# Retention and a gated feed-forward block on one core: start-up laid out by what has landed, filler matmuls, q's squares by way of DRAM, decays per piece, a reordered tail

## The chip, the core and the metric

The kernel runs on one core of a Trainium2 chip. The metric is the device time of one execution in microseconds (us). The kernel before takes 1089.98 us, the median of three runs (1087.69 to 1090.47). One more execution was profiled, and every line of profile below comes from it.

## The reference

All arrays are float32. Eight batches of eight heads, 576 positions, head size 64, go through a decayed causal attention without softmax, and the result, as 4608 tokens of 512 features, goes through a feed-forward block with a gate.

```python
scores = q @ k.T / sqrt(64)
gamma = 1 - 2 ** (-5 - head)
ret = scores * where(i >= j, gamma ** (i - j), 0)
x = (ret @ v)              # heads side by side: (4608, 512)
h = x @ w_in               # w_in (512, 2048)
g = h * erf(softplus(h))
out = g @ w_out            # w_out (2048, 512)
```

## The kernel before, in words

**Attention** works in 40 *pieces*: each batch's 576 positions are cut into four pieces of 128 and one of 64. A piece has three stages. T(i) (`transposes`) turns q and k: TensorE transposes each pair of heads against the identity into PSUM (L296) and ScalarE copies the result out (L297); from the third batch on q comes in an order in which VectorE's 32x32 transpose does q instead (L299). S(i) (`scores`) makes sixteen recorded matmuls (L311) into two PSUM tiles, and VectorE multiplies them by the causal triangle into sT (L92). O(i) (`outputs`) multiplies v by sT (L323), adds q times the running state (L334), and makes the product of k and v for the next state (kv, L346). GpSimd has by then weighed v by powers of gamma (`weigh_values`, L276). VectorE then adds kv to the state and writes the result into the x tile of its chunk, with one operation for each of the four head pairs (L376), because the factor depends on where the piece starts. The state of a batch's first piece is a copy on ScalarE (L358).

The **feed-forward** block works in nine chunks of 512 tokens, four times (g = 0 to 3), each time with 512 of the 2048 hidden features, with a scheme of seven products in place of eight for both layers. Classes `First` (x times w_in, L432) and `Second` (gated result times w_out, L511) hold the seven products in three parts: `first` (two), `middle` (three), `last` (two). Between them stand sums on VectorE: `operands_x` makes four tiles out of a chunk's x, `sums` four out of the gated result, `sums_in` and `sums_out` four out of the weights. ScalarE does softplus (L474) and erf (L479), each with a load of its table ahead of it, and VectorE multiplies (`multiply`).

**Weights** come as 16 parts for each layer (four for each g), 512 KB each, into `wraw` (three buffers). `rounding` is a generator: of one part, a step does two ScalarE operations (L217, L218), then three steps one VectorE operation each (L222, L226, L230), and a fifth one VectorE operation (L235) and two on GpSimd (L236, L237), after which the next part's DMA is issued. After the fourth part of a layer and g come four steps of sums.

**The order is written out by hand**: `manual_schedule` keeps each engine's instructions in program order, so an instruction that waits holds all that follow on its engine. Nearly all DMAs are issued on SyncE's queue (SP), in program order too. `attend` issues the next attention stage, `round_weights(n)` takes n steps of rounding, and `run` walks through a block's products with a stage and a step of rounding after each. The start is: all stages of chunk 0's pieces 0 to 3 (to O(3)), with two steps of rounding after each stage from the second on; `operands_x(0, 0)`; the seven products of chunk 0, two stages after each; then what remains up to O(8), which completes chunk 1; `operands_x(0, 1)`, rounding, and chunk 1's first products. From there on blocks alternate: `First` of chunk n + 1 with `Second` of chunk n, an attention stage after each product as long as there are any. q, k and v of piece i + 3 (q of i + 2) are requested in T(i). From the third batch on `load_squares` requests a batch's q at once, into SBUF, in squares of 32 x 32 (L125), and x of a chunk is stored for the later values of g (L420) at the end of `operands_x`.

Of the kernel before, what the change touches and what calls it, by code (L numbers as in the profile page):

```python
# [22 lines left out]
NS = -(-S // P)  # L23
CONST_COLS = NS * H + NP * P + NS * NP + P

# [6 lines left out]
def decays():  # L32


    gamma = 1.0 - 2.0 ** (-5.0 - np.arange(H, dtype=np.float64))
    pairs = gamma.reshape(2, NP)
    t = np.arange(P)
    starts = np.arange(NS) * P
    gk = pairs.T.reshape(1, 1, H) ** -(starts[None, :, None] + t[:, None, None])
    row = pairs.repeat(D, axis=0)  # L40
    gq = row[:, :, None] ** t[None, None, :] / math.sqrt(D)
    gs = row[:, None, :] ** starts[None, :, None]
    tri = t[None, :] >= t[:, None]
    return np.concatenate([x.reshape(P, -1) for x in (gk, gq, gs, tri)], axis=1).astype(np.float32)
# [3 lines left out]
def kernel(  # L48
# [28 lines left out]
    wraw = ctx.enter_context(tc.tile_pool(name="wraw", bufs=3))  # L77
# [21 lines left out]
    loaded = {i: {} for i in range(len(pieces))}  # L99
# [4 lines left out]

    def load(i, names="kv"):
        if i >= len(pieces):
            return
        b, s0, n = pieces[i]
        for name, src in (("q", q), ("k", k), ("v", v)):
            if name in names and not (name == "q" and b >= SQUARES):  # L110
                bufs = 2 if name == "q" else 4
                t = raw.tile([P, H, D], FP32, tag=name, name=f"raw_{name}", bufs=bufs)
                for e in range(2):
                    heads = src[b, e * NP : (e + 1) * NP, s0 : s0 + n, :]
                    nc.sync.dma_start(out=t[:n, e::2, :], in_=heads.rearrange("h p d -> p h d"))  # L115
                loaded[i][name] = t

    squares = {}

    def load_squares(b):  # L120
        if SQUARES <= b < B:
            t = squares[b] = raw.tile([P, NP, S // SQ, SQ], FP32, tag="q4", name="raw_q4", bufs=2)
# [7 lines left out]
    load(0, "qkv")  # L130
# [3 lines left out]
    for m in (NS * H, NP * P, NS * NP, P):  # L134
        ends.append(ends[-1] + m)
    gk, gq, gs, tri = (cst[:, a:b] for a, b in zip(ends, ends[1:]))
    gk = gk.rearrange("p (s h) -> p s h", s=NS)
    gq = gq.rearrange("p (a i) -> p a i", a=NP)
    load(1, "qkv")
    load(2)  # L140
# [62 lines left out]
    def rounding():  # L203


        while words:
            while words[0][2] > most_g[0]:
                yield
# [34 lines left out]
    for _ in range(3):  # L243
        load_weights()
# [23 lines left out]
    live = {}  # L268
    kept = {}

    def weigh_values(i):

        if i < len(pieces):
            _, s0, n = pieces[i]
            t = loaded[i]["v"]
            nc.gpsimd.tensor_tensor(  # L276
                out=t[:n],
                in0=t[:n],
                in1=gk[:n, s0 // P, :].unsqueeze(2).to_broadcast([n, H, D]),
                op=ALU.mult,  # L280
            )

    def transposes(i):
# [3 lines left out]
        load(i + 2, "q")  # L287
        if s0 == 0:
            load_squares(b + 1)
        weigh_values(i + 1)  # L290
        for name in "qk":
            tT = t[name + "T"] = att.tile([P, NP, P], FP32, tag=name + "T", name=name + "T")
            if name in t:
# [4 lines left out]
            else:  # L298
                nc.vector.transpose(  # L299
                    out=tT[:, :, :n].rearrange("p a (s i) -> p a s i", i=SQ),  # L300
                    in_=squares[b][:, :, s0 // SQ : (s0 + n) // SQ, :],
                )
# [14 lines left out]
    def outputs(i):  # L317
# [24 lines left out]
        if s0 + n < S:  # L342
# [11 lines left out]
            old = kept.get("state")  # L354
            if pieces[i + 1][2] > D:
                new = att.tile([P, NP, D], FP32, tag="state", name="state")
                if s0 == 0:
                    nc.scalar.copy(out=new, in_=kv)  # L358
                else:
                    tt(new, kv, old, ALU.add)  # L360
            else:
                new = states[b % 2]
                for r in heads:
                    tt(new[r, :, r], kv[r], old[r], ALU.add)
            kept["state"] = new
        t0 = b * S + s0
        while t0 < b * S + s0 + n:
# [6 lines left out]
            for p in range(NP):  # L374
                j = s0 // P * NP + p
                nc.vector.scalar_tensor_tensor(  # L376
                    out=x[0, c][:, p, at],
                    in0=o[:, p, a : a + m],
                    scalar=gs[:, j : j + 1],
                    in1=gq[:, p, a : a + m],  # L380
                    op0=ALU.mult,
                    op1=ALU.mult,
                )
# [3 lines left out]
    for i in range(len(pieces)):  # L387
        if i + 1 < len(pieces):
            stages.append((transposes, i + 1))
        stages.append((outputs, i))  # L390
        if i + 1 < len(pieces):
            stages.append((scores, i + 1))
# [17 lines left out]

    def operands_x(g, c):
# [3 lines left out]
        if g == 0:  # L415
# [4 lines left out]
            nc.sync.dma_start(out=xd[c], in_=t)  # L420
# [74 lines left out]
    class Second:  # L495


        def __init__(self, first):
            self.of = first
            self.g, self.c = first.g, first.c  # L500

# [53 lines left out]
        def last(self):  # L555
            self.product(B22, self.a, False)
            self.take(0, 1, self.a, "scalar")
            self.store(0)
            yield
            self.product(T4, self.e, False)  # L560
            self.add(1, 0, self.e)
            self.store(1)
            yield

        def store(self, half):
            if self.g < n_g - 1:
                nc.sync.dma_start(out=od[self.c][:, half], in_=self.o[:, half])
            else:
                r0 = self.c * TCH + half * TH
                nc.sync.dma_start(  # L570
                    out=out[r0 : r0 + TH, :].rearrange("(tp p) o -> p tp o", p=P), in_=self.o[:, half]
# [10 lines left out]

    weigh_values(0)
    while done[0] < stages_for(TCH):
        attend(done[0] + 1)
# [92 lines left out]
```

## Time and profile before

| what | us |
|---|---|
| median of three runs | 1089.98 |
| the profiled execution's own time | 1091.13 |
| its span, first to last instruction | 1089.4 |
| TensorE matmul busy (PE) | 1051.2 (96%) |
| VectorE busy (DVE) | 625.4 (57%) |
| ScalarE busy (ACT) | 397.2 (36%) |
| GpSimd busy (POOL) | 124.7 (11%) |
| mean granted TensorE clock, share of full | 0.987 |
| mean busy share of the 16 DMA engines on the main queue | 51.5% |

PE is busy without a gap from about 123 us to about 1064 us. What a change can win on an engine that is full is not in that stretch; it is ahead of 123 us and after 1064 us. The views used are: the busy time of each engine in stretches of time, with the granted clock; the list of who waited for whom; and the instructions in order of time ("idle before" is how long the engine had stood still, and what released it). PEld is the loading of weights, which lies beside PE.

### The profile page before, as it was taken

To read this page: it belongs to the slowest core of one execution; us is meant where nothing else is said; L and a number is where in the kernel's file an instruction comes from. 1 tells how busy PE (TensorE), PEld (TensorE's weight loads), DVE (VectorE), ACT (ScalarE), POOL (GpSimd) and SP (SyncE) were. 2 spreads that over 40 slices of the span, in tenths; PEclk is the share of its full clock that TensorE was granted. 3 is DMA by queue.
4 is the path that set the end of the run, shared out by engine and by line. 5 is a ranking of instruction groups with operands and counts; after the bars stand their busy time and mean duration, and the time that the engine had idled before them with its cause. 6 is when DMAs were issued, how large, how long until landed. Compare 5 with 4: busy or idle time off the path is not lost.

```text
span 1089.4 us, 15783 instructions
## 1 busy us (share of the span) xinstructions
PE 1051.2 (96%) x6472; PEld 901.3 (83%) x6472; DVE 625.4 (57%) x1074; ACT 397.2 (36%) x501; POOL 124.7 (11%) x110
## 2 busy tenths in 40 slices
PE   4899899999999999999999999999999999999996
PEld 3677788888888888888888888888888888888885
DVE  3738677577667663455555545555655445445444
ACT  2224322414324244433334444333344433333340
POOL 3313221121121000010001100110010000000000
PEclk8989899999999999999999999999999999999999
DMA  9787584665753253355555533555544333444432
GB/s 199 174 187 170 119 223 135 143 191 123 173 165 76 110 193 107 145 184 189 202 201 205 185 149 145 184 193 199 204 187 146 145 145 145 174 181 191 178 116 78
DMA packets 170376, 178.60 MB, mean 164 GB/s; under 512 B 144448, under 2 KB 144448, under 8 KB 162240
## 3 DMA queue, kind: packets, MB, share of 16 engines
q1 hardware_dynamic: 170160, 177.23, 51.5%
q8 instruction: 51, 0.84, 0.3%
q10 hardware_dynamic: 144, 0.36, 0.1%
q14 instruction: 21, 0.17, 0.1%
HBM read 123.30 MB, written 54.26 MB: 163 GB/s over the span
## 4 chain that ended last, share of the span: by engine, by line
PE 92%; DVE 3%; SPq 2%; DMA 2%; POOL 0%; issue 0%; DVEq 0%; POOLq 0%
PE a L511 23%; PE a L432 23%; PE g L511 12%; PE g L432 11%; PE e L432 6%; PE e L511 6%; PE o L323 3%; PE s L311 3%; PE o L334 3%; SPq L115 2%; PE kv L346 2%; PE pt_k L296 1%; DMA raw_q<-in_q_dram 1%; DVE t L92 1%; DMA wraw<-in_moe_w_in_dram 1%
## 5 line engine op out<-in xcount | busy, mean ns | idle before, releaser
L432 PE MATMUL a<-x,wa 128*128 128x256 f32 x1152 | 276.1, 383 | 0.0
L432 PEld LDWEIGHTS a<-x,wa 128*128 128x128 f32 x1152 | 217.4, 191 | 30.6 <-issue 0.4
L511 PE MATMUL a<-wb,s 128*128 128x256 f32 x864 | 205.9, 381 | 2.3 <-DVE o L92 2.3
L511 PEld LDWEIGHTS a<-wb,s 128*128 128x128 f32 x864 | 162.5, 190 | 26.1 <-DVE o L92 2.4
L92 DVE TENSOR_TENSOR t<-g,t 128x512 f32<-128x512 f32 x72 | 49.8, 691 | 159.6 <-ACT t L462 117.6
L432 PE MATMUL g<-x,wa 128*128 128x256 f32 x576 | 137.2, 381 | 0.0
L92 DVE TENSOR_TENSOR o<-a,o 128x512 f32<-128x512 f32 x108 | 74.3, 688 | 108.2 <-PE a L511 105.5
L432 PEld LDWEIGHTS g<-x,wa 128*128 128x128 f32 x576 | 108.2, 190 | 14.8
L236 POOL TENSOR_TENSOR wraw<-wraw 128x512 f32<-128x512 f32 x32 | 34.0, 1064 | 548.2 <-DVE wraw L235 312.6
L457 ACT COPY t<-a 128x512 f32<-128x512 f32 x36 | 21.1, 586 | 194.0 <-PE a L432 194.0
L92 DVE TENSOR_TENSOR t<-t,s 128x1024 f32<-128x1024 f32 x72 | 85.0, 1221 | 0.0
L474 ACT ACTIVATE s<-t 128x1024 f32<-128x1024 f32 x72 | 72.1, 1048 | 29.3 <-DVE t L92 29.3
L511 PE MATMUL e<-wb,t 128*128 128x256 f32 x288 | 69.7, 385 | 4.9 <-POOL wb L237 4.9
L468 ACT COPY t<-a 128x512 f32<-128x512 f32 x36 | 21.1, 586 | 143.1 <-PE a L432 143.1
L479 ACT ACTIVATE s<-s 128x1024 f32<-128x1024 f32 x72 | 72.1, 1049 | 0.4
L511 PE MATMUL a<-wb,t 128*128 128x256 f32 x288 | 68.6, 381 | 1.9 <-DVE t L92 1.9
L432 PE MATMUL e<-x,wa 128*128 128x256 f32 x288 | 70.2, 388 | 0.0
L511 PE MATMUL g<-wb,t 128*128 128x256 f32 x288 | 68.6, 381 | 0.0
L511 PE MATMUL g<-wb,s 128*128 128x256 f32 x288 | 68.5, 380 | 0.0
L276 POOL TENSOR_TENSOR raw_v<-raw_v,cst 128x512 f32<-128x512 f32 (+1 forms) x40 | 49.1, 1231 | 158.0 <-DMA raw_v<-in_v_dram 114.8
L511 PEld LDWEIGHTS e<-wb,t 128*128 128x128 f32 x288 | 54.6, 192 | 12.8 <-POOL wb L237 5.3
L511 PEld LDWEIGHTS a<-wb,t 128*128 128x128 f32 x288 | 54.1, 190 | 9.7 <-DVE t L92 2.3
(59 smaller groups left out, 1200.5 us busy)
## 6 DMA issues: line engine op xcount, KB each, us to landing
x<-xd SPq DMA_DIRECT2D x27, 1792.0 KB, 11.0
od<-o SPq DMA_DIRECT2D x54, 512.0 KB, 3.9
o<-od SPq DMA_DIRECT2D x27, 1024.0 KB, 7.3
xd<-x SPq DMA_DIRECT2D x9, 1792.0 KB, 6.5
out_dram<-o SPq DMA_DIRECT2D x18, 512.0 KB, 2.8
raw_k<-in_k_dram SPq DMA_DIRECT2D x64, 128.0 KB, 3.6
raw_v<-in_v_dram SPq DMA_DIRECT2D x64, 128.0 KB, 3.2
wraw<-in_moe_w_in_dram SPq DMA_DIRECT2D x32, 256.0 KB, 4.7
```

Of the source, the lines that this page charges most:

```text
L92: nc.vector.tensor_tensor(out=out, in0=in0, in1=in1, op=op)
L115: nc.sync.dma_start(out=t[:n, e::2, :], in_=heads.rearrange("h p d -> p h d"))
L236: nc.gpsimd.tensor_tensor(out=r_f, in0=high_f, in1=r_f, op=ALU.mult)
L276: nc.gpsimd.tensor_tensor(out=t[:n], in0=t[:n], in1=gk[:n, s0 // P, :].unsqueeze(2).to_broadcast([n, H, D]), op=ALU.mult,)
L311: nc.tensor.matmul(ps[e][:n, p, :n], lhsT=t["kT"][r, p, :n], rhs=t["qT"][r, p, :n], start=True, stop=True)
L323: nc.tensor.matmul(o[e * D : (e + 1) * D, p, :n], lhsT=t["v"][:n, 2 * p + e, :], rhs=t["sT"][:n, e, p, :n], start=(p == 0), stop=(s0 == 0 ...
L334: nc.tensor.matmul(o[r, p, :n], lhsT=kept["state"][r, p, :], rhs=t["qT"][r, p, :n], start=False, stop=(p == NP - 1), skip_group_check=True,)
L346: nc.tensor.matmul(kv[e * D : (e + 1) * D, p, :], lhsT=t["k"][:n, 2 * p + e, :], rhs=t["v"][:n, 2 * p + e, :], start=(p == 0), stop=(p == ...
L432: nc.tensor.matmul(acc[:, j * TH : (j + 1) * TH], lhsT=weights["wa", self.g][:, a, d, j * P : (j + 1) * P], rhs=x[self.g, self.c][a][:, d, :],
L474: nc.scalar.activation(self.s[:, j], t, AF.Softplus)
L479: nc.scalar.activation(self.s[:, j], self.s[:, j], AF.Erf)
L511: nc.tensor.matmul(acc[:, tp, :], lhsT=left[:, j * TH + tp * P : j * TH + (tp + 1) * P], rhs=weights["wb", self.g][:, b, j, :], start=(sta ...
```

## The change

What it does, in the order of the diff:

- **Decays relative to the piece.** The factors for v no longer depend on the piece's start. The state is multiplied by gamma to the 128th (`gp`) at each piece instead: for a first piece on VectorE in the place of ScalarE's copy, for the others VectorE adds kv to the state (`sums`) and GpSimd multiplies, with two GpSimd operations of 64 partitions ahead of a half piece. In return the result of a piece goes into x with one VectorE operation in place of four. The constants shrink from 683 to 652 columns. `weigh_values(i + 1)` moves from T(i) to O(i), after the state.
- **Loads.** q, k and v of pieces 0 to 3 are requested at the start, ahead of the first weights, q with four buffers; `wraw` has four buffers in place of three, and four parts are requested.
- **q's squares by way of DRAM.** A batch's squares are written to a DRAM tile by four DMAs, and each piece's q is loaded from there (256 KB) as q of the first two batches is. The DMAs of a batch are issued at the second piece of the batch before.
- **Filler matmuls.** `keep_busy(n)` issues n matmuls of the identity with itself into a PSUM tile that nobody reads: 9 at the very start, 2 after each of the first six stages, and 14 between the first and second products of chunk 0 (35 in all).
- **Rounding** moves: five steps each after T(3), O(2) and O(3), five and four around chunk 0's first two products, two after each stage from T(6) to O(8), six in chunk 1's first products.
- **Stages.** After chunk 0's last piece O(3) comes ahead of T(4). In chunk 0's products no stage follows the first two, and one in place of two the other five. What remains up to O(8) follows chunk 0's last product and `erf`, without products between.
- **Stores of x** move out of `operands_x` to a little later.
- **Tail.** In the last block but one `multiply` goes ahead of `last`; of the last chunk's output the second half's right columns are stored before the last product, and the left ones after it.

```diff
-    def load(i, names="kv"):
...
-    def load_squares(b):
+    def make_squares(b):
         if SQUARES <= b < B:
-            t = squares[b] = raw.tile([P, NP, S // SQ, SQ], FP32, tag="q4", name="raw_q4", bufs=2)
+            t = squares[b] = dram.tile([P, NP, S // SQ, SQ], FP32, tag="sq", name="sq", bufs=B)
...
+    def load(i):
+        if i >= len(pieces) or i in loaded or i in live:
+            return
+        b, s0, n = pieces[i]
+        t = loaded[i] = {}
+        for name, src in (("q", q), ("k", k), ("v", v)):
+            t[name] = raw.tile([P, H, D], FP32, tag=name, name=f"raw_{name}", bufs=4)
+            if name == "q" and b >= SQUARES:
+                t[name] = t[name].rearrange("p h d -> p (h d)").rearrange("p (a i) -> p a i", a=NP)
+                nc.sync.dma_start(
+                    out=t[name][:, :, :n].rearrange("p a (s d) -> p a s d", d=SQ),
+                    in_=squares[b][:, :, s0 // SQ : (s0 + n) // SQ, :],
+                )
+                continue
...
-    load(1, "qkv")
-    load(2)
+    for i in range(1, 4):
+        load(i)
...
-    for _ in range(3):
+    for _ in range(4):
         load_weights()
...
         load(i + 3)
-        load(i + 2, "q")
-        if s0 == 0:
-            load_squares(b + 1)
-        weigh_values(i + 1)
+        if s0 == P:
+            make_squares(b + 1)
...
+            half = pieces[i + 1][2] == D
+            sums = kv
+            if s0 > 0:
+                sums = att.tile([P, NP, D], FP32, tag="sums", name="sums")
+                tt(sums, kv, kept["state"], ALU.add)
+            if half:
                 new = states[b % 2]
                 for r in heads:
-                    tt(new[r, :, r], kv[r], old[r], ALU.add)
+                    nc.gpsimd.tensor_tensor(out=new[r, :, r], in0=sums[r], in1=gp[r], op=ALU.mult)
+            else:
+                new = att.tile([P, NP, D], FP32, tag="state", name="state")
+                (nc.gpsimd if s0 > 0 else nc.vector).tensor_tensor(out=new, in0=sums, in1=gp, op=ALU.mult)
             kept["state"] = new
+        weigh_values(i + 1)
...
-            for p in range(NP):
-                j = s0 // P * NP + p
-                nc.vector.scalar_tensor_tensor(
...
+            tt(x[0, c][:, :NP, at], o[:, :, a : a + m], gq[:, :, a : a + m], ALU.mult)
             t0 += m
...
     for i in range(len(pieces)):
...
+        stages += [(transposes, i + 1), (outputs, i), (scores, i + 1)]
+        if i == TCH // P - 1:
+            stages[-3:-1] = stages[-2], stages[-3]
...
             self.store(0)
+            if self.end:
+                self.store(1, slice(OH, D_MODEL))
             yield
             self.product(T4, self.e, False)
             self.add(1, 0, self.e)
-            self.store(1)
-            yield
+            self.store(1, slice(0, OH if self.end else D_MODEL))
+            yield
...
+    idle = ps_e.tile([P, W], FP32, tag="g", name="idle")
+
+    def keep_busy(n):
+        for _ in range(n):
+            nc.tensor.matmul(idle[:, :P], lhsT=ident, rhs=ident, start=True, stop=True)
+
+    keep_busy(9)
     weigh_values(0)
-    while done[0] < stages_for(TCH):
-        attend(done[0] + 1)
-        if done[0] >= 2:
-            round_weights(2)
+    for j in range(stages_for(TCH)):
+        attend(j + 1)
+        if j < 6:
+            keep_busy(2)
+        if j in (8, 9, 11):
+            round_weights(5)
     operands_x(0, 0)
...
-    run(firsts[0].first(), (0, 1), 2)
-    run(firsts[0].middle(), (0, 1, 2), 2)
-    run(firsts[0].last(), (0, 1), 2)
+    steps = firsts[0].first()
+    next(steps)
+    round_weights(5)
+    keep_busy(14)
+    next(steps)
+    round_weights(4)
+    run(firsts[0].middle())
+    run(firsts[0].last())
+    store_x(0)
     firsts[0].erf()
     most[0] = stages_for(3 * TCH) - 1
-    attend(stages_for(2 * TCH))
+    while done[0] < stages_for(2 * TCH):
+        attend(done[0] + 1)
+        round_weights(2)
     operands_x(0, 1)
-    round_weights(4)
-    run(firsts[1].first(), (0, 1))
+    store_x(1)
+    run(firsts[1].first(), (3, 3))
     firsts[0].multiply()
-    round_weights(4)
...
             seconds[n + 1].begin()
             run(b.middle())
+            firsts[n + 1].multiply()
             run(b.last())
-            firsts[n + 1].multiply()
             firsts[n + 1].sums()
             run(nxt.first())
```

## Prediction

> **What bounds the kernel now.** First the busy shares of the page: matmuls hold 96% of the span, so what counts is where they do not. Then the busy time in stretches of 5 us (length, then busy time and count of PE, PEld, DVE, ACT, POOL; then PE's granted clock, DMA share, GB/s):
>
> ```profile
> 15.00:20.00 5.00, 1.05 (x10) 1.05 (x12) 2.52 (x8) 3.27 (x7) 0.00 (x0) 0.80 1.05 234
> 20.00:25.00 5.00, 1.05 (x11) 0.79 (x9) 4.28 (x7) 0.29 (x1) 3.36 (x3) 0.50 1.18 180
> ...
> 55.00:60.00 5.00, 5.00 (x30) 4.13 (x30) 2.48 (x7) 0.16 (x1) 0.00 (x0) 0.66 0.98 278
> ...
> 110.00:115.00 5.00, 2.79 (x10) 1.97 (x12) 2.75 (x6) 0.00 (x0) 2.07 (x2) 0.52 0.80 169
> ```
>
> The loss is of two kinds: standing still (span 1089.4 less 1051.2 busy: 38.2 us), and matmuls at half the clock after it (busy time times one less the clock, summed over the slow stretches up to 120 us: some 9 us). The list of waits names the first kind:
>
> ```profile
> PE pt_q L296 <- DMA raw_q<-in_q_dram: 11.3, 3, 5.2
> PE s L311 <- ACT kT L297: 6.4, 2, 5.7
> PE e L511 <- POOL wb L237: 4.9, 1, 4.9
> PE a L511 <- DVE o L92: 2.3, 3, 0.8
> ...
> PE a L511 <- DVE t L92: 1.9, 1, 1.9
> ```
>
> The order of time says when and why. (Start, duration, engine, line, operation; in brackets the idle time before and who ended it.)
>
> ```profile
> 16.73 0.66 ACT L217 ACTIVATE wa<-wraw 128x512 f32<-128x512 f32 x1 [8.62 <-DMA wraw<-in_moe_w_in_dram]
> ...
> 18.95 2.08 PE L311 MATMUL s<-qT,kT 64*128 64x128 f32 x16 [5.72 <-ACT kT L297]
> ...
> 22.27 0.95 DVE L222 TENSOR_SCALAR wa<-wa 128x512 f32<-128x512 f32 x1
> ...
> 24.98 1.09 PE L296 MATMUL pt_q<-ident,raw_q 128*128 128x128 f32 x4 [3.95 <-DMA raw_q<-in_q_dram]
> ```
>
> The copy of kT that S(1) needs stood on ScalarE behind a rounding step that waited for its weights; q of piece 2 had been requested behind the weights. The chunk's first product starts at 42.27, its second at 48.70 (3.58 long, slow), its third at 56.69; chunk 1's third at 92.93. The 4.9 us fall at 107.3 to 112.2, for rounded w_out, and the last waits lie in the tail, 1063 us on.
>
> **What the Trainium skill says.** "TensorE: Matmul & The Clock Gate", What's actually happening: after an idle window of about 3.4 us the array runs at half clock, until about 3.4 us of work have passed. The trace agrees: S at 18.95 takes 2.08 where a warm one takes 1.16, and it is warm again at 28.55, 3.6 us after work resumed; but a wait of 2.19 us at 75.8 was enough to slow it too. "GPSIMD Engine Reference", Key points: GpSimd shares SBUF interfaces with VectorE, which collides with VectorE operations in a two-port mode or with two SBUF inputs. The trace agrees: L222 above, 0.43 alone, took 0.95 beside GpSimd, and one weighing (1.04) took 4.19 at 97.45. "DMA: Bandwidth & Descriptors", Two DMAs through the same engine are not ordered: a DMA that reads what another wrote must be preceded by a wait for its semaphore on the issuing engine. The kernel before has no such pair for q; here SP waits for a batch's four writes ahead of the first read.
>
> **The change part by part.** Warm prices from the rows: T 1.1, S 1.09, O 2.65 (1.63 for a batch's first piece), a half piece 0.8, 0.7 and 2.0, a product 1.73 from start to start. On DVE sT is 1.28, a 512-wide sum 0.69, kv 0.42, a part's four rounding operations 0.43 + 0.43 + 0.69 + 0.43 = 1.98, `operands_x` 2.61; a part's two on POOL are 1.04 + 1.28 = 2.32. GpSimd's multiply of the state is not in the trace: half of 1.04 to all of it; I take 0.6.
>
> *To O(3).* Fillers: 9 end at about 3.9 us (0.27 each cold), ahead of q at 5.17, and are free; the pairs (0.27 to 0.54) lie in waits for loads. Pieces land every 3.7 us (786 KB at the 213 GB/s of 5 to 20 us), so attention runs through to O(2), about 23.5 us. The first part of weights, 16.7 before, now has q(2) and all of piece 3 ahead of it, 1.05 MB: 21.4; the second 24. Their rounding stands on DVE ahead of sT(3): ScalarE to 25.3, DVE's end 26.9, sT(3) 28.2. So O(3) waits 3.7 us, starts cold (+1.7) and ends near 32.7, where before it ended at 42.3. The 5.7 and 3.95 us waits are gone; **what is late next is rounding.**
>
> *Chunk 0.* Part 2's and 3's DVE steps stand behind O(3): 0.42 + 0.69 + 1.98 + 2.61 + 1.98 on DVE, then 2.32 on POOL: 10.0. The second product starts at about 42.9, with one product and 14 fillers (0.135 each, 1.9 us) in between; a gap of over 6 us is left, so it is cold, 3.6 us, to 46.5. Three sums of 0.69 stand ahead of the third: 48.6. That is 8.1 us earlier than 56.7, but T(4), S(4), T(5), O(4), S(5), which lay in before's waits (0.8 + 0.7 + 1.1 + 2.0 + 1.1 = 5.7), are still to do: **2.4 us ahead**.
>
> *To chunk 1's third product.* Before: 36.2 us, of which 30.3 is work and 5.9 loss. Now: 36.0 of work, and these losses. A second cold spell, 1.7. Then kT(6) stands on ScalarE behind softplus and erf of chunk 0: after the seventh product 0.7 + 2.0 + 1.3 + 2.0 + 1.2 = 7.2 until it is copied, while PE has S(5), T(6), O(5), 3.9: a wait of 3.2, and 1.3 of cold clock. Then attention alone: from O(i) to O(i+1) DVE has kv, x, the rest of a rounding part and sT, 0.42 + 0.69 + 1.1 + 1.28 = 3.5, PE only S and T, 2.2: 1.3 for each of O(6), O(7), O(8), and 1.1 for T(7), whose PSUM waits for x(5). Sum 1.7 + 3.2 + 1.3 + 5.0 = 11.2. 48.6 + 36.0 + 11.2 = 95.8, **2.9 behind** 92.9.
>
> *To 123 us.* w_out is rounded beside that stretch, so 4.9 us of waiting and 2.6 of cold clock (112 to 118) go: 7.5. What is late next is DVE: after O(8) it has about 15.4 us up to sT(10), and PE 15.2 up to O(10): 0 to 3, I take 1.5. **3.1 ahead.**
>
> *Steady work.* Per piece DVE loses 4 x 0.28 = 1.1 and gains 0.69; POOL gains 0.6 (two such before a half piece); PE nothing. After kv, sums (0.42), state (0.6) and weighing (1.04) make 2.1, and the next O is a product, S and another away, 4.5 or more: hidden; with a rounding part ahead on POOL 2.3 more, at the limit. q by DRAM adds 7 MB to 178 at half-used engines; between zero and, if SP stands at the squares with k and v behind, a load's 4 us each batch. T's loads are requested three pieces ahead, so zero. SP's stores of x and later weights have slack. The smaller constants, 16 KB, are nothing. ScalarE loses 8 x 0.37, off the path.
>
> *Tail.* `multiply` (2.35) can start when erf ends (1064.8), not after T4's sum (1069.0): the 1.92 us wait before the last chunk goes, and the sums behind it come earlier: the third product at 1072.3 for 1074.7, **2.4**. The chain after it is the same. The last store is 256 KB in place of 512: at 205 GB/s at most 1.2 less, but the first half's 512 KB and the right columns lie ahead on the same engines; nothing to 1.2, I take 0.3.
>
> Sum: 3.1 + 2.4 + 0.3 = 5.8. The profiled execution's own time is 1091.13 (span 1089.4 and 1.7 around it): 1085.3. The median of the runs shown is 1.15 below that execution: **1084.2**.
>
> **The rivals.** *Warm* (27%): fillers and shorter gaps keep the clock at full. Against it stands a 6 us gap after the 14; for it, that a filler costs nothing where PE would stand. The four cold terms go, 1.7 + 1.9 + 1.7 + 1.3 = 6.6: 1077.6. *Given back* (15%): the stall for w_out is gone, but DVE, in order, is as late with q's transpose, sT and the gated product after O(8) as POOL was with w_out, and 5 of the 7.5 are lost there: 1089.2. *Collision* (13%): the other side. With all rounding packed into the start, DVE's chains lie beside GpSimd's: at 22.27 such a chain took 3.4 us in place of 1.98. If it does so for every part on the path (part 1 ahead of sT(3), 2 and 3 ahead of the second product, four of w_out in attention alone), that is 7 x 1.4 = 9.9: 1094.1. It evens out the gain from about four such parts, and is slower by 0.3% from between six and seven. That the fillers don't run as meant is not open: they wait for the identity alone.
>
> **How the numbers follow.** The forecast, 1080 to 1088, has 45%. About 0.3%, 3.3 us, is what can be told from no change, so faster is below 1086.7: seven eighths of the forecast's and all of *warm*, 66%. Slower is above 1093.2: most of *collision* and of an unseen loss, 13%. The rest, 21%, is the same. The range takes in *warm* with half of its waits gone as well, and *given back*: 1074 to 1092.5, with a tenth left out on each side. The bounds of the unknown costs (0 to 3 after O(8), 0 to 1.2 at the end) lie within.
>
> **What would show it.** Right: no wait for ACT kT before O(3), the chunk's first product near 33 and its second near 43 us behind POOL wa; S(6) waiting for ACT kT near 70; waits of about 1.3 us for DVE sT up to 90; none for POOL wb; PE full from about 110; no wait for DVE t in the tail. Wrong: a first product later than 36 us or a second earlier than 40; a clock of 1.00 between 40 and 75; waits of PE between 125 and 400 us, or SP standing at the squares.

## The result and the profile after

The changed kernel takes 1091.97 us, the median of 4 runs (1091.08 to 1094.55), beside 1090.06 for the kernel before in 4 runs (1087.69 to 1090.47): a ratio of 1.0026 [1.0004, 1.0048]. It is slightly slower, by 2 to 3 us (1.9 by the medians, 2.8 by the ratio); the forecast was 1084.2, 7.8 us too low. The profiled execution of the changed kernel took 1094.55 (span 1092.8), 3.4 more than that of before, and 2.6 more than its own median; the times below come from it. Some of its loss is its own: the traces of e2, e4 and e9, experiments that start in nearly the same order, reach chunk 1's third product at 102.6 to 103.8, where this one has 105.99.

First the stretches of 5 us, with the columns that the prediction shows:

```profile
15.00:20.00 5.00, 5.00 (x78) 4.47 (x76) 1.65 (x4) 1.07 (x2) 0.32 (x1) 1.00 0.83 178
20.00:25.00 5.00, 4.90 (x72) 4.07 (x72) 3.45 (x8) 3.04 (x6) 1.29 (x2) 1.00 1.02 255
25.00:30.00 5.00, 0.41 (x8) 0.22 (x4) 4.90 (x7) 1.77 (x3) 4.60 (x4) 0.79 1.07 187
...
40.00:45.00 5.00, 1.39 (x9) 0.79 (x7) 4.90 (x7) 0.00 (x0) 2.92 (x2) 0.99 0.25 81
45.00:50.00 5.00, 1.29 (x3) 1.11 (x4) 1.10 (x2) 0.00 (x0) 3.66 (x4) 0.50 0.28 81
...
55.00:60.00 5.00, 5.00 (x19) 3.65 (x18) 0.00 (x0) 1.33 (x3) 0.00 (x0) 0.52 0.35 79
...
110.00:115.00 5.00, 5.00 (x45) 4.22 (x40) 4.93 (x9) 1.13 (x2) 0.00 (x0) 1.00 0.92 273
```

From 15 to 25 us TensorE (the first pair) is now full at full clock, where before it worked a fifth of the time; from 110 it is full too. Between lie new holes, at 25 and at 40 to 50. In the first two of them VectorE (third pair) has 4.90 of 5.00 and GpSimd (fifth pair) 4.60 and 2.92: both are busy together while TensorE stands. TensorE's waits name the new causes:

```profile
PE o L318 <- POOL raw_v L279: 7.7, 3, 5.4
PE e L424 <- POOL wa L240: 7.3, 2, 5.0
PE s L306 <- ACT kT L297: 3.3, 2, 3.1
PE a L424 <- DVE x L90: 2.5, 1, 2.5
PE a L424 <- DVE wa L90: 2.2, 1, 2.2
PE a L504 <- DVE o L90: 2.1, 3, 0.8
PE idle L583 <- POOL ident masks.py:199: 1.4, 1, 1.4
```

The 11.3 us for q, the 5.7 for kT, the 4.9 for rounded w_out and the 1.9 for t in the tail are gone. In their place stand waits for VectorE's and GpSimd's work on the first weights. The order of time:

```profile
22.23 0.67 ACT L220 ACTIVATE wa<-wraw 128x512 f32<-128x512 f32 x1 [0.26 <-DMA wraw<-in_moe_w_in_dram]
...
25.14 1.04 POOL L239 TENSOR_TENSOR wraw<-wraw 128x512 f32<-128x512 f32 x1 [3.85 <-DVE wraw L238]
...
25.85 0.61 DVE L225 TENSOR_SCALAR wa<-wa 128x512 f32<-128x512 f32 x1
26.26 1.35 POOL L240 TENSOR_TENSOR wa<-wa,wraw 128x512 f32<-128x512 f32 x1
...
26.49 1.40 DVE L229 TENSOR_SCALAR wa<-wa 128x512 uint32<-128x512 uint32 x1
...
27.58 0.79 POOL L360 TENSOR_TENSOR state<-sums,cst 128x256 f32<-128x256 f32 x1
27.93 0.98 DVE L233 SCALAR_TENSOR_TENSOR wa<-wraw,wa 128x512 uint32<-128x512 uint32 x1
28.33 1.49 POOL L279 TENSOR_TENSOR raw_v<-raw_v,cst 128x512 f32<-128x512 f32 x1
28.95 1.15 DVE L238 TENSOR_SCALAR wraw<-wa 128x512 uint32<-128x512 uint32 x1
...
30.02 1.27 DVE L90 TENSOR_TENSOR sT<-s,cst 128x512 f32<-128x512 f32 x2
...
39.73 4.41 DVE L90 TENSOR_TENSOR x<-x 128x512 f32<-128x512 f32 x4
...
41.39 1.60 POOL L240 TENSOR_TENSOR wa<-wa,wraw 128x512 f32<-128x512 f32 x1
```

ScalarE takes up the first weights at 22.23, as forecast (21.4). But VectorE's L229 and L238, 0.43 each when nothing runs beside them, take 1.40 and 1.15 under GpSimd's L240 and L279. Part 1's four rounding operations last from 25.85 to 30.1, 4.2 us where the forecast has 1.98; sT(3) stands behind them in VectorE's order, and O(3) behind sT(3).

The ends of these rows show what the longer times are made of. L225, L229 and L238 end at 26.46, 27.89 and 30.10, each 0.28 us after the GpSimd instruction that was running when they started (26.18, 27.61, 29.82); L233, with two inputs, ends at 28.91, 0.54 after the state's 28.37. So VectorE's four operations go in step with GpSimd's four. That reads as a wait for the end of a running GpSimd instruction, and not as a slower pace of VectorE; the last section counts such rows over ten traces.

(The list puts O(3)'s wait down to raw_v, whose weighing ended at 29.82; sT's first half ended just ahead of O(3)'s start at 30.80.) The four sums of `operands_x` take 4.41 in place of 2.61. In TensorE's order of time:

```profile
30.80 2.52 PE L318 MATMUL o<-sT,raw_v 128*64 128x128 f32 x16 [5.39 <-POOL raw_v L279]
...
43.05 0.70 PE L424 MATMUL e<-x,wa 128*128 128x256 f32 x2 [2.36 <-POOL wa L240]
48.71 2.93 PE L424 MATMUL e<-x,wa 128*128 128x256 f32 x6 [4.96 <-POOL wa L240]
53.84 2.45 PE L424 MATMUL a<-x,wa 128*128 128x256 f32 x8 [2.20 <-DVE wa L90]
...
77.21 1.16 PE L306 MATMUL s<-qT,kT 64*128 64x128 f32 x16 [3.08 <-ACT kT L297]
...
80.92 2.47 PE L318 MATMUL o<-sT,raw_v 128*64 128x128 f32 x16 [0.64 <-DVE sT L90]
...
89.80 1.64 PE L318 MATMUL o<-sT,raw_v 128*64 128x128 f32 x16 [1.49 <-POOL raw_v L279]
...
95.54 1.39 PE L318 MATMUL o<-sT,raw_v 128*64 128x128 f32 x16 [0.82 <-POOL raw_v L279]
```

Chunk 0's third product starts at 53.84 (before 56.69), but chunk 1's third only at 105.99 (before 92.93), after a 2.53 us wait for sums that took 4.60. Five marks hold the whole comparison (us, from the traces and the prediction; the last forecast is 123.34 less 3.1; "layer two" is the first product of `wb` with s, the first that comes after the old stall for w_out):

| start of | before | forecast | after | e10 |
|---|---|---|---|---|
| chunk 0, first product | 42.27 | 32.7 | 35.57 | 36.96 |
| chunk 0, third product | 56.69 | 48.6 | 53.84 | 56.35 |
| chunk 1, first product | 88.13 | - | 98.49 | 85.74 |
| chunk 1, third product | 92.93 | 95.8 | 105.99 | 93.42 |
| layer two | 123.34 | 120.2 | 129.37 | 118.40 |

From layer two on, TensorE is full in both kernels up to the tail, where 2.4 us come back. 6.0 behind less 2.4 and 0.2 (the last store) is the 3.4 by which the spans differ.

### The profile page after: what moved, and what is told of

It reads as the page before. It is cut to its first block, busy times and chain, and to the rows that moved or that the text cites. A ratio compares the mean times of both kernels' runs of the same rounds, so it can differ in the third digit from the quotient of the medians.

```text
span 1092.8 us, 15842 instructions
## 1 busy us (share of the span) xinstructions
PE 1060.7 (97%) x6542; PEld 910.7 (83%) x6542; DVE 615.3 (56%) x942; ACT 394.5 (36%) x493; POOL 148.4 (14%) x142
## 4 chain that ended last, share of the span: by engine, by line
PE 92%; DVE 3%; SPq 1%; DMA 1%; ACT 1%; POOL 1%; issue 1%; DVEq 0%; POOLq 0%
PE a L424 23%; PE a L504 23%; PE g L424 12%; PE g L504 12%; PE e L424 6%; PE e L504 6%; PE o L318 3%; PE o L329 3%; PE s L306 3%; PE kv L341 1%; SPq L131 1%; PE pt_k L296 1%; DVE x L90 1%; DMA wraw<-in_moe_w_in_dram 1%; DMA raw_k<-in_k_dram 0%
## 5 line engine op out<-in xcount | busy, mean ns | idle before, releaser
L449 ACT COPY t<-a 128x512 f32<-128x512 f32 x36 | 21.1, 586 | 204.8 <-PE a L424 204.8
L90 DVE TENSOR_TENSOR t<-t,s 128x1024 f32<-128x1024 f32 x72 | 88.0, 1262 | 0.0
L460 ACT COPY t<-a 128x512 f32<-128x512 f32 x36 | 21.1, 586 | 151.1 <-PE a L424 151.1
L424 PEld LDWEIGHTS e<-x,wa 128*128 128x128 f32 x288 | 54.8, 193 | 15.6 <-POOL wa L240 7.9
L90 DVE TENSOR_TENSOR sT<-s,cst 128x512 f32<-128x512 f32 (+1 forms) x80 | 47.0, 627 | 31.7 <-PE s L306 31.6
L454 ACT COPY t<-a 128x512 f32<-128x512 f32 x36 | 21.1, 586 | 109.7 <-PE a L424 109.7
```

The lines of the kernel that those rows point to most:

```text
L90: nc.vector.tensor_tensor(out=out, in0=in0, in1=in1, op=op)
L424: nc.tensor.matmul(acc[:, j * TH : (j + 1) * TH], lhsT=weights["wa", self.g][:, a, d, j * P : (j + 1) * P], rhs=x[self.g, self.c][a][:, d, :],
L449: nc.scalar.copy(out=self.t1[:, 1], in_=self.a)
L454: nc.scalar.copy(out=self.t2[:, 1], in_=self.a)
L460: nc.scalar.copy(out=self.t2[:, 0], in_=self.a)
```

## The experiments

All ratios are to the kernel before, run beside each version, with a 95% interval; its median there was 1089.3 to 1090.3.

**e1, the tail alone**: the kernel before with only the two edits at the end (`multiply` ahead of `b.last()`, the split last store).

> The kernel before with the tail alone changed (multiply ahead of the last products of the last block but one; the last store split). By every theory the tail is worth what the two traces show: the matmuls end 2.4 us earlier, the store gives 0 to 0.5. So 2.4 to 2.9 us less than before (about 1087.4), the start as before. If the tail's gain were an accident of where the changed kernel stood, it would be under 1.

1086.52 us (11 runs), 0.9972 [0.9963, 0.9981]. By its ratio it is 3.1 us faster than before, against the 2.7 of the forecast's tail and store, and it beats both kernels. So the rest of the change costs 5 to 6 us instead of gaining 3.

**e2, no fillers**: `keep_busy` does nothing.

> The changed kernel without its 35 filler matmuls. If the fillers hold the clock up, the start to O(2) is slower (half-clock S, T, O up to about 11 us as before) and the total 1 to 3 us above the changed kernel. Collision theory (the start is set by VectorE and GpSimd getting in each other's way, TensorE waits for them): within 0.7 us of the changed kernel, since every filler lies in a wait.

1092.87 us (20 runs), 1.0027 [1.0016, 1.0037]; chunk 0's second and third products start at 43.10/48.77 and 53.89 as with fillers. The 35 matmuls of the identity cost nothing and gain nothing that can be measured.

**e3, the rounding's GpSimd pair on VectorE** for the first group:

```
+            on = nc.vector if g == 0 else nc.gpsimd
-            nc.gpsimd.tensor_tensor(out=r_f, in0=high_f, in1=r_f, op=ALU.mult)
-            nc.gpsimd.tensor_tensor(out=a_f, in0=a_f, in1=r_f, op=ALU.add)
+            on.tensor_tensor(out=r_f, in0=high_f, in1=r_f, op=ALU.mult)
+            on.tensor_tensor(out=a_f, in0=a_f, in1=r_f, op=ALU.add)
```

> The changed kernel with the last two operations of each rounding part moved from GpSimd to VectorE while g is 0 (eight parts, start only). Collision theory: GpSimd no longer slows VectorE's operations (a part's four took 3.1 to 4.2 us in place of 1.98, the four sums of x 4.4 and 4.6 in place of 2.6), so although VectorE gets 2 x 0.69 more for each part, chunk 0's second product comes 2 to 4 us earlier than 48.7, and the total falls by 2 to 5 us. Rival, order alone (VectorE's queue is simply too long, whoever stands beside it): each part is 1.4 longer on VectorE, the second product comes no earlier, the total rises by 1 to 4 us.

1099.44 us (4 runs), 1.0084 [1.0064, 1.0104]: slower, and by more than the 1 to 4 us of the rival. The expected gain did not come: 8 parts x 2 operations x 0.69 put 11 us on VectorE, in whose order the path lies, and chunk 0's second product started at 45.73 and 51.77 in place of 43.05 and 48.71. Its VectorE lines in order of time show the prices all the same:

```profile
24.36 0.43 DVE L229 TENSOR_SCALAR wa<-wa 128x512 uint32<-128x512 uint32 x1
...
28.85 1.15 DVE L229 TENSOR_SCALAR wa<-wa 128x512 uint32<-128x512 uint32 x1
...
45.59 2.61 DVE L90 TENSOR_TENSOR x<-x 128x512 f32<-128x512 f32 x4
```

GpSimd had nothing at 24.36 and nothing after 44.4, and the four sums took 2.61 again; at 28.85 it had a weighing, which ended at 29.71, and L229 ended 0.29 after it.

**e4, chunk 0's sums behind part 3's rounding** on VectorE, so that part 3 comes to GpSimd sooner:

```
-    operands_x(0, 0)
+    operands_x(0, 0, (0,))
...
     round_weights(5)
+    operands_x(0, 0, (1,))
     keep_busy(14)
```

> The changed kernel with chunk 0's four sums of x behind the rounding of part 3 in place of ahead of it (the second product doesn't need them). Theory that the second product is late because of what stands ahead of its weights on VectorE: it comes about 4.4 us earlier (near 44.3); the third product needs the sums, and comes at most 1 to 2 us earlier, as the sums now stand ahead of it. Total 0 to 2.5 us less than the changed kernel. Rival, TensorE's half clock decides: the shorter gap keeps the array warmer, 3 us or more less.

1091.03 us (20 runs), 1.0016 [1.0009, 1.0023]. The second product came at 43.38/47.57, 1.1 us sooner for its last six matmuls, and not near 44 (the third product, 1.2 sooner, and the total lie within the expected range): part 3's rounding now lay under GpSimd's part 2 (3.65 us) and the sums under part 3 (5.26 us). Swapping two VectorE jobs only moves which of them collides.

**e5, stages between chunk 0's products**, as the kernel before has them, and **e6, also in the first gap**:

```
 e5, e6:
-    run(firsts[0].middle())
-    run(firsts[0].last())
+    run(firsts[0].middle(), (4, 4, 4), 2)
+    run(firsts[0].last(), (4, 4), 2)
 e6:
-    keep_busy(14)
+    attend(done[0] + 4)
```

> The changed kernel with two attention stages in place of one after each of chunk 0's products 3 to 7, as in the kernel before, and four rounding steps with each (the same 22 steps in all before chunk 1). Order theory (the start loses because attention and rounding run with no product between them, so that TensorE waits for VectorE's queue): S(6)'s wait for kT behind erf goes (3.1 us) and the waits of O(6) to O(8) shrink; chunk 1's third product comes 4 to 7 us after what 105.99 was, less; total 1085 to 1088. Load theory (VectorE's work in the start is what sets the time, wherever it stands): within 1.5 us of the changed kernel.

> As the run with two stages a product, and the four stages T(4), S(4), T(5), O(4) in place of the 14 fillers between chunk 0's first and second product. Order theory: the 7.3 us wait of the second product is filled with 4.6 us of work that is done later otherwise: another 2 to 5 us less, total 1081 to 1086. Load theory: the second product comes later by what the stages put on VectorE ahead of it, and the total stays within 1.5 us of the run with two stages a product.

1093.61 us (5 runs), 1.0048 [1.0033, 1.0063], and 1093.9 us (5 runs), 1.0046 [1.0029, 1.0062]: taken as they ran, both speak against the order theory, whose ranges were 1085 to 1088 and 1081 to 1086. The trace of e6 says otherwise. VectorE and SyncE's queue in order of time:

```profile
89.28 0.41 DVE L90 TENSOR_TENSOR x<-o,cst 128x256 f32<-128x256 f32 x1
...
92.84 0.59 SPq L399 DMA_DIRECT2D xd<-x  x1
...
102.55 0.42 DVE L90 TENSOR_TENSOR x<-o,cst 128x256 f32<-128x256 f32 x1 [12.85 <-DMA xd<-x]
```

In e6 chunk 1's first two products were ahead of before (86.29 for 88.13). Then VectorE stood 12.85 us: the x pool has two buffers, and chunk 2's x takes chunk 0's, which is free only when its store has landed. The change moved that store behind chunk 0's last product, and in e6 the loads and weights that the added stages and rounding steps request stand ahead of it in SyncE's order, so it was issued at 92.84; the rest of VectorE's order, chunk 1's sums among it, stood behind, and TensorE waited 14.4 us. e5 has the same wait, 7.1 us on VectorE and 5.8 on TensorE. In the changed kernel itself the store is issued at 68.3 and VectorE does not wait for it. So e5 and e6 tested two things at once. A third differs as well: as the code stands, 32 rounding steps lie ahead of chunk 1's sums in e5, not the 22 of the changed kernel that e5's text gives; in e6 it is 24.

**e7 and e8, two parts by themselves**, on top of e1: the decays relative to the piece (the state multiplied in place on GpSimd, `weigh_values` left in T), and q's squares by way of DRAM.

> The kernel before with the tail and the decays per piece alone (state multiplied in place, by GpSimd from a batch's second piece on; one VectorE operation a piece into x). Both theories of the start: VectorE's work per piece falls by 0.4 us, GpSimd's grows by 0.6, in a start where VectorE's queue is on the path for some eight pieces: 0 to 3 us less than before with the tail alone (1086.5). Collision rival: GpSimd's extra multiply beside VectorE gives it back, 0 to 2 us more.

> The kernel before with the tail and q's squares by way of DRAM alone. If the way by DRAM is hidden (as forecast): within 0.8 us of before with the tail alone (1086.5). If SP stands at a batch's squares with k and v behind it, or the extra 14 MB of traffic delays the loads of the start: 1 to 4 us more.

1087.52 us (14 runs), 0.9985 [0.9977, 0.9993], and 1087.56 us (13 runs), 0.9983 [0.9975, 0.9991]. e1's ratio is 0.9972, taken at another time. By the ratios each is 1.2 to 1.4 us above it (e8's text allowed 0.8), and the intervals overlap; neither gains by itself, and neither alone explains the 5 to 6 us.

**e9, the early store alone**, and **e10, e6 with the early store**:

```
     operands_x(0, 0)
+    store_x(0)
...
     run(firsts[0].last())        (in e10 with the stages of e6)
-    store_x(0)
```

> The changed kernel, with one line moved: the store of chunk 0's x stands right behind its operand sums, where the kernel before had it, instead of behind chunk 0's last product. Whole output. In e5 and e6 VectorE stood 5.8 and 12.9 us on this store, since chunk 2's x takes the buffer that it frees; in the changed kernel's own trace VectorE shows no idle time there. If the moved store costs only where products and stages are mixed, this gives the changed kernel's time, 1091 to 1092; if the late store already delayed it (by delaying other transfers in SyncE's queue), 2 to 5 us less: 1087 to 1090.

> e6 (T(4), S(4), T(5), O(4) in place of the 14 fillers, two stages and four rounding steps behind each of chunk 0's products 3 to 7) with the store of chunk 0's x right behind its operand sums. Whole output. Order theory: what the change loses is the covered order; e6 had chunk 1's first two products 1.8 us ahead of the kernel before and lost it in one wait of 14.4 us for that store. Without the wait chunk 1's third product comes near 91 (before 92.9), and with the 7 us regained later and the tail's 2.4 the time is 1078 to 1083. Rival, the prices: VectorE beside GpSimd can't prepare chunk 1's operands sooner in whatever order; the third product stays near 102 to 106 and the time 1089 to 1094.

e10: 1082.58 us (6 runs), 0.9932 [0.9919, 0.9946], **7.4 us faster than before**, 9.4 faster than the changed kernel, and 11.3 faster than e6, from which it differs by the place of one store. Chunk 1's third product is at 93.42. That is at the upper edge of what the order theory said (1078 to 1083, the product near 91), and far from the rival's 1089 to 1094. e9: 1095.78 us (6 runs), 1.0052 [1.0035, 1.007], where 1087 to 1092 was expected. Its runs spread from 1091.2 to 1098.7, and the trace is of the shortest (span 1089.4), so it does not show where the longer ones lost time. Their mean granted clocks fall as the times rise: 0.992 at 1091.2, 0.989 at 1092.6, 0.986 at 1095.7 to 1096.1, 0.981 at 1098.7. The interval overlaps that of the changed kernel. At least the early store alone gains nothing in the changed kernel's order. e10's largest waits of TensorE up to 140 us:

```profile
PE o L318 <- POOL raw_v L279: 7.6, 2, 6.5
PE o L318 <- DMA wraw<-in_moe_w_out_dram: 5.1, 1, 5.1
PE a L424 <- DVE x L90: 2.7, 1, 2.7
PE a L424 <- DVE wa L90: 2.1, 1, 2.1
```

The start is not better than in the changed kernel: the first two lines are O(3) and O(4), which wait for sT behind rounding on VectorE whatever releaser the list names, and chunk 0's third product starts 2.5 us later than after (with four stages more done). What differs comes later. From chunk 0's third product to chunk 1's third, in before, after and e10 (length, then busy time and count of PE, PEld, DVE, ACT, POOL; clock, DMA share, GB/s):

```profile
56.69:92.93 36.24, 33.57 (x334) 27.64 (x333) 17.02 (x43) 15.18 (x23) 5.40 (x5) 0.92 0.69 145
```

```profile
53.84:105.99 52.15, 43.25 (x405) 34.64 (x405) 28.20 (x45) 20.66 (x33) 17.33 (x16) 0.87 0.73 164
```

```profile
56.35:93.42 37.07, 33.28 (x348) 27.50 (x349) 26.70 (x44) 20.03 (x31) 16.41 (x15) 0.95 0.81 162
```

VectorE does nearly the same work in e10 as after (26.70 and 28.20), GpSimd too, but in 37 us instead of 52. TensorE stands 3.8 us instead of 8.9 (length less busy), and loses 1.7 instead of 5.6 to the clock (busy times one less the clock). These make 9.0 of the 15.1 us between the two stretches; the other 6.0 is TensorE work that e10 had done ahead of its stretch.

**e11, meant to put chunk 0's erf behind S(6)**, on top of e10, so that piece 6's kT is copied first:

```
-    firsts[0].erf()
+    late = stages.index((scores, 6)) + 1
     while done[0] < stages_for(2 * TCH):
         attend(done[0] + 1)
+        if done[0] == late:
+            firsts[0].erf()
```

> e10 with chunk 0's erf behind the scores of piece 6 instead of ahead of the remaining attention, so that ScalarE copies piece 6's kT first and TensorE doesn't wait 3.1 us for it. Whole output. If that wait lies on the path in this order, 1 to 3 us less than e10; if chunk 1's sums end it anyway, the same as e10 within 0.7 us.

1082.77 us (6 runs), 0.993 [0.9917, 0.9944]: the same as e10. But the edit does not do what its text says. In e10's order S(6) stands behind one of chunk 0's products, so it is done before this loop begins, the condition is never met, and the kernel leaves out chunk 0's erf: its profile counts 70 such instructions (x70), e10's 72:

```profile
L471 ACT ACTIVATE s<-s 128x1024 f32<-128x1024 f32 x70 | 70.1, 1049 | 0.4
```

So no move was tested. That leaving out 2.0 us of ScalarE's work, and the load of its table, gains nothing says that chunk 0's erf holds up nothing in e10, where no S waits for kT from chunk 0's third product on.

**e12 and e13, e10's two halves**, each with the early store: only the stages behind products 3 to 7, and only the four stages in the first gap.

> e10 without its first half: the 14 fillers stand again between chunk 0's first two products, in place of T(4), S(4), T(5), O(4); two stages and four rounding steps stay behind each of chunk 0's products 3 to 7, and the store of chunk 0's x stays early. Whole output. Four stages that e10 has between the first two products are then left over for behind the last product, alone. If it is the number of stages with a product between them that counts, four fewer lose about a third of e10's gain over the changed kernel: 1084 to 1087. If the stages behind products 3 to 7 are all that counts, 1081 to 1084. If the first gap was the gain, 1088 to 1092.

> e10 without its second half: T(4), S(4), T(5), O(4) in place of the 14 fillers, the store of chunk 0's x early, but chunk 0's products 3 to 7 bare as in the changed kernel and the other stages behind the last one. Whole output. If the number of covered stages counts, a third of the gain: 1087 to 1089. If the stages behind products 3 to 7 are all that counts, the changed kernel's time or more, 1091 to 1096. If the first gap was the gain, 1082 to 1085.

e12: 1086.55 us (15 runs), 0.9977 [0.9967, 0.9987]. e13: 1085.08 us (5 runs), 0.9962 [0.9949, 0.9975]. Against e9 (1.0052), either half takes back some 8 to 10 us, and the second one another 3 to 5; against the changed kernel itself (1.0026) it is 5 to 7. They are not additive. e12 lies in the range for the number of covered stages (1084 to 1087), e13 at the edge of that for the first gap (1082 to 1085) and below the count's 1087 to 1089, so none of the three explanations fits both. Chunk 1's third product is at 98.53 in e12, at 96.40 in e13. The two differ in more than the stages: ahead of chunk 1's sums e12 has 32 rounding steps, e13 14, e10 24 and the changed kernel 22. How much of e13's gain comes of rounding put off to later is open.

**e14, without the rounding's GpSimd pair** for the first group, in the changed kernel's own bare order:

```
+            if g > 0:
-            nc.gpsimd.tensor_tensor(out=r_f, in0=high_f, in1=r_f, op=ALU.mult)
-            nc.gpsimd.tensor_tensor(out=a_f, in0=a_f, in1=r_f, op=ALU.add)
+                nc.gpsimd.tensor_tensor(out=r_f, in0=high_f, in1=r_f, op=ALU.mult)
+                nc.gpsimd.tensor_tensor(out=a_f, in0=a_f, in1=r_f, op=ALU.add)
```

> The changed kernel without the two GpSimd operations that end a part's rounding (their multiply and their addition), for the first group's eight parts; the products wait for VectorE's operations instead. The low part of the first group's weights is left out. The order is the changed kernel's. A lower bound on what these two cost: collision with VectorE and their own 2.3 us behind it. Collision theory: VectorE's chains and sums go back to the prices they have alone (four rounding operations 2.0 in place of 3.1 to 4.2, four sums 2.6 in place of 4.4 to 4.6), GpSimd's 2.3 goes too: chunk 0's second product whole near 42 to 43.5, its third near 47 to 48.5, chunk 1's third 6 to 9 us earlier than 106, and 1083 to 1087 in all. If the bare order is the loss whatever the prices, what is gained at the start is lost again in the attention that is left alone: chunk 1's third product at 102 or later, 1088 to 1091.

1084.69 us (5 runs), 0.9949 [0.9935, 0.9962], as the collision theory expected, and not the 1088 to 1091 of the bare order alone; the start came less far than it said (second product at 40.76/45.49, third at 49.94), since the state and the weighing still collide. O(3) is hardly sooner (30.28 for 30.80), but this execution's first weights came 0.9 us later. Its order of time:

```profile
28.43 0.69 DVE L233 SCALAR_TENSOR_TENSOR wa<-wraw,wa 128x512 uint32<-128x512 uint32 x1
29.15 0.43 DVE L238 TENSOR_SCALAR wraw<-wa 128x512 uint32<-128x512 uint32 x1
...
40.58 3.33 DVE L90 TENSOR_TENSOR x<-x 128x512 f32<-128x512 f32 x4
...
45.49 2.25 PE L425 MATMUL e<-x,wa 128*128 128x256 f32 x6 [4.13 <-DVE wa L233]
...
49.94 3.50 PE L425 MATMUL a<-x,wa 128*128 128x256 f32 x8 [2.20 <-DVE wa L90]
```

Part 1's L238 is back at 0.43, and the sums take 3.33 instead of 4.41. Chunk 1's third product starts at 98.93, 7.1 us sooner than in the changed kernel: 3.9 of it are there by chunk 0's third product (GpSimd's own 2.3 us behind the last part among them), 3.2 come in the attention after it. Of the 7.1, some 2 us belong to the one execution of the changed kernel that was traced: 98.93 is 4.6 to 4.9 sooner than in e9's and e2's traces.

## Why the prediction was wrong, step by step

- **The start, to O(2).** Right. O(2) ended at 24.3 (forecast 23.5), the first weights came at 22.23 and 24.28, and no kT waits behind a rounding step.
- **O(3).** The step "ScalarE to 25.3, DVE's end 26.9, sT(3) 28.2" failed by its term for one part's four operations: 4.2 us measured for 1.98, each waiting for the GpSimd instruction beside it. It left out GpSimd's own order too: the weighing that O(3) needs now stands behind part 0's pair and the state. From 25.14 that is 1.04 + 1.28 + 0.6 + 1.04, an end at 29.1 even at the prices alone, later than 28.2. O(3) ended at 35.57 instead of 32.7, 2.9 late.
- **Chunk 0's second product.** The sum "0.42 + 0.69 + 1.98 + 2.61 + 1.98 on DVE, then 2.32 on POOL: 10.0" measured 13.1 (35.57 to 48.66): the sums 1.8 more, part 2's chain 1.1 more. Six of its eight matmuls started at 48.71 instead of 42.9. Two did not wait for part 3, which the forecast had not seen, but that led to nothing. The 14 fillers took 3.29 us instead of 1.9, inside the wait.
- **Chunk 0's third product.** 53.84 for 48.6, the same 5.2 carried on. The 2.4 ahead was gone by here: 2.9 sooner than before, with the same 5.7 us of stages still to do.
- **To chunk 1's third product.** The forecast's 36.0 of work and 11.2 of loss measured 37.6 and 14.5 (8.9 standing, 5.6 clock). Some of the work was there to be read: before's stretch, by its line above, has 30.9 of work and 5.4 of loss, where the prediction took 30.3 and 5.9. S(6)'s wait was right (3.08 for 3.2). The three waits for sT were smaller, 2.95 in all where the step had 5.0 with T(7)'s. Cold clock was larger, in part by this one execution (the stretch is 52.15 us long here and 49.9 in e2's trace), and one wait was not in the sum: chunk 1's four sums, 4.60 long beside GpSimd, with 2.53 us of TensorE behind them.
- **To 123 us.** Right in kind, low in size: 13.1 behind became 6.0 behind, 7.0 regained where 7.5 less 1.5 was said. No wait of TensorE for wb is left.
- **Steady work and the tail.** Right: TensorE is full from 140 to 900 us in both, the tail gave 2.4 and the store 0.2 (0.3). SyncE did stand for the squares, 19.0 us in ten waits, the longest 3.5, but TensorE did not wait. The constants went from 700 columns (not 683) to 652, 24 KB less instead of the prediction's 16, which changes nothing.

So the mechanisms were seen, and most of their order; the prices failed. Of the signs that the prediction named for being wrong, the two at the start did not come (a first product after 36 us, a second before 40). The page that the prediction cites, "GPSIMD Engine Reference", Key points, names the collision; the prediction quoted 0.95 for 0.43 and then priced every chain as if VectorE were alone. The trace of before held more: that L222 ended at 23.22, 0.28 after GpSimd's L237, which ran 1.28 us from 21.66. *Collision*, given 13%, put 9.9 us on seven parts, and the trace shows 10.2 us more than the forecast at chunk 1's third product, but that is luck: the excess was not 1.4 in each part but 2.3, 1.1 and 0.1 in parts 1 to 3, and 1.8 and 2.0 us are in operand sums that this rival did not name. e14, without the pair, comes to 1084.69, near the forecast; that is partly chance, as it leaves out GpSimd's own 2.3 us too.

The prices are one part of the cause. e10 keeps them (part 2's chain and chunk 0's sums take 3.1 and 4.41 in it as well) and is 9.4 us faster than the changed kernel. The other part is the **bare order**: packed into the start and then into attention by itself, rounding has no product beside it, so what VectorE and GpSimd take from each other is on the path at once; with two stages and four rounding steps behind each product most of it is covered. The two are no shares of one sum: e10 mends the order alone and e14 thins out the collision alone, and each ends 7 to 9 us below the changed kernel. e12 and e13 show that a part of the cover is enough to end faster than before. The prediction had this in its own words ("then attention alone") and priced it as one set of small waits.

What stays open: why e9 took longer than the changed kernel, beyond its lower clock; what the move of the weighing behind the state costs, which no run has by itself; how the 4 us between e1 and e10 divide among the earlier weights, w_out's rounding and the new start, which was not tried; and whether the collision by itself, with GpSimd's work done but elsewhere in SBUF, would give e14's gain.

## What to carry to other kernels

Price an operation by the company that the new order gives it, not by its fastest instance: here a rounding operation of VectorE that started under a GpSimd instruction ended after it, so both engines' orders have to be laid side by side. Before stages are taken out from between large products and put side by side, sum what the engines in order have to do there; the work is as long as before, but nothing covers it. When an order is tried, check which stores free the buffers that it needs sooner: one late store here hid 11 us of gain. And look in the trace whether an edit did what it was meant to: e11's did not, and its time did not tell.

## What the runs showed of the hardware

- Beside GpSimd, VectorE's rounding operations waited. In ten of the traces (before, after, e2, e3, e4, e9, e10, e12, e13, e14), up to 140 us, 80 of the 81 with one input that started while a GpSimd instruction ran ended 0.27 to 0.35 us after it, and 25 of the 27 with two inputs 0.53 to 0.56 after it (counted in the order of time, rows of one instruction alone). So what one loses depends on how much of the GpSimd instruction is left: L229 took up to 1.45 (e13) for 0.43, L233 up to 1.65 (e4) for 0.69, about 1 us more each.
- It goes the other way as well: the three exceptions lie under two weighings of the kernel before, at 97.45 and 104.55, and there VectorE's rows kept their prices while the weighings took 4.19 and 1.59 in place of 1.04.
- The Trainium skill, "VectorE: DVE Perf Modes", Mode 2×_2P — use both read ports for one tensor, says that a single-source fp32 operation from SBUF takes both read ports and so runs at twice the rate, and "GPSIMD Engine Reference", Key points, counts that mode among those that collide. The trace agrees: alone, the one-input L225 takes 0.43, well under the 0.69 of the two-input L233 of the same size, and both waited for GpSimd.
- Four 512-wide sums took 2.61 alone and 3.33 to 5.26 beside GpSimd (up to 2.0 times).
- GpSimd's L240, beside those sums, took 1.60 at 41.39 and 1.28 alone.
- The versions scatter differently: e2 from 1089.6 to 1096.6 in 20 runs, e9 from 1091.2 to 1098.7 in 6, e14 from 1083.8 to 1085.9 in 5, and the kernel before from 1087.6 to 1091.4 in the 47 that ran beside e2. Why is not shown.
